# Two pairs of late token tiles multiplied in seven half-width products instead of eight

## The chip, the cores and the metric

The kernel runs on one core of a Trainium2 chip. The metric is the device time of one execution in microseconds (us). Before the change the median of three runs is 405.96 us (405.43 to 406.44). A profiled execution, with its trace, lies beside them.

## The reference

Eight batches of 576 tokens pass two stages. The first is attention through 32 packed queries, with 8 heads of 64 columns: `packed = softmax(p k^T / 8) v`, then `out = softmax(q packed^T / 8) packed`. The second is a gated feed-forward layer on the 512 columns that the heads make together:

```python
h = np.maximum(x @ w_in, 0.0)                  # 512 -> 1024
conv_out = sum(conv_w[k] * hp[:, k:k + S, :])  # three neighbouring tokens, per column
gate = 1.0 / (1.0 + np.exp(-conv_out))
return h * gate @ w_out                        # 1024 -> 512
```

The last line is the second layer. The change is in that product alone: 4608 tokens by 1024 columns of `h * gate`, times `w_out` of 1024 by 512. Results are float32, and q, k, p and `conv_w` are drawn eight times larger than plain random numbers.

## The kernel before

**Precision.** TensorE multiplies rounded float32 (`F32R`). Each operand x of a product is split into `hi`, x rounded, and `lo`, x minus `hi`. A product is three matmuls into one PSUM tile: hi by hi, lo by hi, hi by lo. ScalarE (ACT) writes `hi`, VectorE (DVE) writes `lo`.

**First layer.** `ffn1(b, j)` (L645) computes 128 of the 1024 columns for batch b: 12 matmuls of 288 columns (L666) into a `big` PSUM tile, of which there are three. Then ACT and DVE take turns on 576 tokens: relu out of PSUM (L678), the convolution's middle tap (L682), its two outer taps (L684, L688 on DVE), tanh (L692) and the gating (L694 on DVE), which leaves `hgt[b % 2][:, j]`.

**Second layer.** `ffn2(m)` (L715), for each of the 36 tiles of 128 tokens: ACT and DVE convert the tile's 1024 columns of `hgt` into `xhi` and `xlo` (L705, L708), PE takes 8 steps of three matmuls of 512 columns (L757), ACT copies the PSUM tile to `o` (L765) and SP's queue stores it (L767). There are two `x` pairs and two `o` tiles. The PSUM tile is `fo`, or `sm` for odd m from 31 on. The last tile is done in two halves of 256 columns, `sm` and then `fo`. Tiles 29 and 30 hold tokens of batch 6 alone, tile 31 of batches 6 and 7, tiles 32 to 35 of batch 7 alone.

**Order.** Each function is a stream of steps, one step for one engine. `ORDER` is a fixed string of two-character stream numbers: `Flow.run` (L156) takes them in turn and emits the next step of that stream. So the order of the instructions on each engine is fixed by the string, and the engines meet only at semaphores. The planner's times in the steps decide nothing here except how many idle matmuls fill the start. Tiled steps (AV, scores, `packed_weight`) use parts of the array, the others all of it.

Of the kernel before, what the change touches and what calls it, by code (L numbers as in the profile page):

```python
# [26 lines left out]
    "1a0u1n0m0u124f6e1n451l4d4e4f6e0u454f4d1a4h1c4e4e0u0u4f4g1b0y1k4d451b4i4f4f114j4i7e1n7e4k4i6e1g4h6f4j6e6e4i6f6e4k"  # L27
    "4h4k4i4j4i7f161i121a4k4j4i6e1i6f6f121e1a4j4k4l7f1d126f6f6f6f4j4k4l1i6f1o4k6g121s4l1i4l6g4h124l7g4m1a4l6f1a1j4m1q"
    "191j1i1a6f4m4j121i6g1q7g1w6g6h6e4n6g4m6h1q204n1a1v6g1i6g4m1v4l1h6g4m1a4n124m121r1v4n6g6g236f7h1a6g4o121i4n1i4o4p"
    "6h6h4o4p4p1a236h124o7h4o6h4n1q6g4p1a6h6h6h4p6h4o1m4o1a1y4n234p4p1q1i6h1i1q4q282b1y4r6i1r1y6i1y1a1i6i126i6i1q1a2b"  # L30
    "4r6i12241a4q4q1z6i6j1a6i1a4r1i6i6i4s6i2b1p4s6j4s1q4t4u1q4s1i1y1i4t4s264t1t4t1q1z6k1y2g6j2c4u6j1y4u4s261i6j2j4u6j"
    "4s6k6j264u2j4v4t2j1q6j271i4u1u4v226i4u6j266j4t2e1x4w2k6j4t1i4v1q2e1i1q6k4w2e4v2a1i1q6h2f2e4v3p6k6k6k4w1y1i274x26"
    "6k1q6k6l1y4x6l216k6k6k2f4x1q6k4x2m1y4v50266m1q6l6l4w264v1q2r2m6l2h4w6l2m2r506l4x2r6l4y4w1q4y291y6l6l4w501q4y6l6m"
    "4z6m4z262o2n4x1q6m4z2e6m4y6m6m2z1y4x4z6m264y4y4z524z1y4y52524z6l6m251y522s6m34536n535354542e6m2m542e26512u526n6n"
    "6o6n546j6n261y516n532z54526n2z6n6n6n52541y376n516o376p5554553753536m6o262u6o2w552e5630266o6o55266o5635535655266o"
    "6o57552n5756551y56566o2i6p6o1y586p262u6p586q562e596p262d58596p6p6n596p2m6p1y586p6q58576p2m2e6o2u57595a1y5732592m"
    "6q2l1y58586q57266q596q6q3232572m3f2m6q362q6q592e266r6q5b6q262m6r3f2e265a5b6r6r6s6p6r6r5a5c2m6r6s2e5d6r6r5c2e6r5c"
    "5d2m5b5c5c5d5e6r2m6s2e5c6s5e325c5f2u2e5d5e5e6r5d5d383f5e5f2e6s5f5e336s6s6t2v5f6s6s2e6t5k3a2m5d2p2u6s5f5f6s5k5g6t"
# [146 lines left out]
def tile_packed_attention_conv_gate(  # L185
# [15 lines left out]
    HG = 4  # L201
# [17 lines left out]
    MOVED = 10  # L219

# [7 lines left out]
    stage = cpool.tile([128, 2 * DFF], F32, name="stage")  # L228
    cw_raw = cpool.tile([3 * NJ, 128], F32, name="cw_raw")
    cw = cpool.tile([128, 3 * NJ], F32, name="cw")  # L230
    w_in_sb = cpool.tile([128, NCC, DFF], F32, name="w_in_sb")
# [8 lines left out]
    vfree = [cpool.tile([128, HG, SV + 1, D], F32, name=f"v{i}") for i in range(2)]  # L240
# [3 lines left out]
    def warm(n):  # L244
# [6 lines left out]
        | dict(gw=2, h=3, x=2, o=2),  # L251
# [4 lines left out]
    def big():  # L256
        return ps.tile([128, 2, 512], F32, name="big", tag="big", bufs=3)

# [230 lines left out]

    afree = [stage[:, i * (SV + 1) * 128 : (i + 1) * (SV + 1) * 128] for i in range(2)]  # L490

    def attention(g):
# [12 lines left out]
        if g >= MOVED:  # L505
            yield Step("DVE", 1230, after=[("wp", 2), ("wp", 5)], take=["ad"], give=["a1"])
# [28 lines left out]
        yield Step("PE", 640, after=[("v", g)], take=["sm"], give=["a1T", "v"], cols=960, tiled=True)  # L535
# [12 lines left out]
        vfree.append(G["v"])  # L548
        yield Step("ACT", 251, after=[("rs", g)], take=["pb"], give=["sm"], sets=[("pb", g)])
# [10 lines left out]
        yield Step("PE", 556, after=[("qT", g)] + [("s2", g - 1)] * (g > 0), take=["big", "s2"], give=["qT"], sets=[("s2", g)], cols=1152, tiled=True)  # L560
        t = score(ppT, G["qT"], g)
        yield Step("DVE", 665, give=["big"])
# [41 lines left out]
    def packed_weight(b, hf):  # L604
# [3 lines left out]
        yield Step("PE", 905, after=after, take=["big", "gw"], give=["ppT"] * NG if hf else (), sets=[("pk", i)], cols=2048, tiled=True)  # L608
        t = big()
        for i in range(NG * HG):  # L610
# [11 lines left out]
            )  # L622
        yield Step("ACT", 904)
# [18 lines left out]

    hfree = list(hbuf)

    def ffn1(b, j):  # L645
# [3 lines left out]
        if b >= 2:  # L649
            after += [("x", m) for m in tiles_of(b - 2)]  # L650
# [64 lines left out]
    def ffn2(m):  # L715
        bs = range(m * 128 // S, ((m + 1) * 128 - 1) // S + 1)
        halves = m < HALVED
        last = NJ // 2 if halves else NJ
        after = [("hg", b, j) for b in bs for j in range(last)]
        if m:  # L720
            after.append(("x", m - 1))
        yield Step("ACT", 520 if halves else 947, after=after, take=["x"])
        hi = wk.tile([128, NJ, 128], F32R, name="xhi", tag="xhi")
        lo = wk.tile([128, NJ, 128], F32R, name="xlo", tag="xlo")
        cuts = []
        for b in bs:
            s0, s1 = max(m * 128, b * S), min((m + 1) * 128, (b + 1) * S)
            cuts.append((hgt[b % 2][:, :, s0 - b * S : s1 - b * S], slice(s0 - m * 128, s1 - m * 128)))
        split[m] = hi, lo, cuts
        yield from convert(m, slice(0, last), [("xa" if halves else "x", m)])  # L730
        bank = "sm" if m > NTT - 6 and m % 2 else "fo"
        parts = 2 if m == NTT - 1 else 1
        banks = ("sm", "fo") if parts == 2 else (bank,)
        for n in range(NJ * parts):
            q, c = divmod(n, NJ)
            fs = slice(q * DM // parts, (q + 1) * DM // parts)
            end = n == NJ * parts - 1
            after = [("w", 4 + c // 2)]
            if n == 0 and m:
                after.append(("fo", m - 1))  # L740
            if c == last:
                after.append(("x", m))
# [6 lines left out]
                give=["x"] if end else (),  # L749
# [3 lines left out]
            if c == 0:  # L753
                t = small(banks[q])
                sums_of[m, q] = t
            for i, (x, w) in enumerate(((hi, wo_hi), (lo, wo_hi), (hi, wo_lo))):
                nc.tensor.matmul(  # L757
                    out=t[:, : fs.stop - fs.start], lhsT=x[:, c, :], rhs=w[:, c, fs], start=c + i == 0, stop=c == NJ - 1 and i == 2
                )
        yield from store(m, fs, q, banks[q])  # L760

    def store(m, fs, q, bank):
# [4 lines left out]
        nc.sync.dma_start(out=out.rearrange("b s f -> (b s) f")[m * 128 : (m + 1) * 128, fs], in_=o[:, fs])  # L767

# [21 lines left out]
    for m in range(NTT):  # L790
        flow.add(ffn2(m))
# [34 lines left out]
```

## Time and profile before

| | us |
|---|---|
| median of three runs | 405.96 |
| the profiled execution's own time | 408.01 |
| its span, first to last instruction | 406.2 |
| PE busy | 395.3 (97%) |
| DVE busy | 339.9 (84%) |
| ACT busy | 275.5 (68%) |

The profile is one execution. PE is TensorE's matmuls, PEld its weight loads, SPq the queue of transfers that SP issues. A matmul's shown duration overlaps the next one's start, so what one costs is read from start to start. Every mean granted clock is 1.000, which is 2.4 GHz. The chain of waits follows the work back from the last instruction, and before the last store it is PE alone from 369 us on. Three things are to be kept apart: how long PE's own work is, what PE waited for, and how far ahead of it DVE and ACT were.

### The profile page before, as it was taken

Reading aid. Unit: us, or ns where it says so; the run is one execution under the profiler, and the core shown is the slowest. Engines: PE = TensorE matmul, PEld = TensorE weight load, DVE = VectorE, ACT = ScalarE, POOL = GpSimd, SP = SyncE. Lnnn points to the kernel's source line nnn. Section 1 sums busy time; section 2 is a strip of 40 time slices with the busy share of each in tenths; the row PEclk is TensorE's granted clock in tenths of the full one; section 3 lists DMA queues with packets and bytes.
Section 4 is the critical chain, followed back from the end, with each engine's and each line's share of the span. In section 5 each row is a group of like instructions: output and inputs, shape, how many; then the busy total and the mean of one; then the engine's idle time right before and its main releaser. Section 6 shows DMA issues by size and latency. Waiting matters only on the chain.

```text
span 406.2 us, 8244 instructions
## 1 busy us (share of the span) xinstructions
PE 395.3 (97%) x3321; PEld 316.9 (78%) x3321; DVE 339.9 (84%) x494; ACT 275.5 (68%) x475; POOL 1.6 (0%) x16
## 2 busy tenths in 40 slices
PE   7899899999999999999999999999999999999996
PEld 5768576778868878888779788788687878887886
DVE  0699989999999999999999999999889886557220
ACT  3889899977777586776666765677665676655231
POOL 1000000000000000000000000000000000000000
PEclk9999999999999999999999999999999999999999
DMA  8999989999758787397473715416001001010211
GB/s 295 363 353 209 319 225 176 134 155 158 111 92 118 118 192 142 73 190 113 92 114 102 148 54 102 129 31 114 28 2 52 27 6 47 26 53 0 77 53 52
DMA packets 140377, 49.19 MB, mean 121 GB/s; under 512 B 121244, under 2 KB 132788, under 8 KB 140340
## 3 DMA queue, kind: packets, MB, share of 16 engines
q1 hardware_dynamic: 140340, 48.67, 54.5%
q8 instruction: 26, 0.43, 0.5%
q14 instruction: 11, 0.09, 0.1%
HBM read 37.25 MB, written 9.44 MB: 115 GB/s over the span
## 4 chain that ended last, share of the span: by engine, by line
PE 79%; DMA 10%; DVE 5%; SPq 3%; ACT 2%; issue 1%; ACTq 0%
PE fo L757 42%; PE big L666 20%; DMA v<-in_v_dram 4%; PE sm L757 3%; PE big L453 3%; DMA hgt<-in_moe_w_in_dram 3%; PE big L614 3%; SPq L520 2%; PE sm L539 2%; DMA p<-in_p_dram 1%; PE big L331 1%; PE big L530 1%; DMA out_dram<-o 1%; DVE hgt L684 1%; DVE hgt L688 1%
## 5 line engine op out<-in xcount | busy, mean ns | idle before, releaser
L757 PE MATMUL fo<-wo_hi,xhi 128*128 128x512 f32 (+1 forms) x272 | 109.8, 404 | 0.7 <-ACT o L765 0.7
L757 PE MATMUL fo<-wo_lo,xhi 128*128 128x512 f32 (+1 forms) x272 | 106.5, 391 | 0.0
L757 PE MATMUL fo<-wo_hi,xlo 128*128 128x512 f32 (+1 forms) x272 | 106.1, 390 | 0.0
L757 PEld LDWEIGHTS fo<-wo_hi,xhi 128*128 128x128 f32 x272 | 51.2, 188 | 15.7 <-issue 3.0
L678 ACT ACTIVATE hbuf<-big 128x576 f32<-128x576 f32 x64 | 41.7, 657 | 31.5 <-PE big L666 31.4
L684 DVE SCALAR_TENSOR_TENSOR hgt<-hbuf,cw,hgt 128x576 f32<-128x576 f32 x64 | 51.3, 806 | 13.4 <-ACT hgt L682 13.0
L757 PEld LDWEIGHTS fo<-wo_lo,xhi 128*128 128x128 f32 x272 | 51.1, 188 | 12.3
L708 DVE TENSOR_TENSOR xlo<-hgt,xhi 128x1024 fp32r<-128x1024 f32 (+1 forms) x44 | 44.7, 1021 | 16.7 <-ACT xhi L705 16.6
L757 PEld LDWEIGHTS fo<-wo_hi,xlo 128*128 128x128 f32 x272 | 51.1, 188 | 8.6
L666 PE MATMUL big<-a2hi,ghi 128*128 128x288 f32 x256 | 55.7, 299 | 0.0
L692 ACT ACTIVATE hgt<-hgt 128x576 f32<-128x576 f32 x64 | 43.7, 688 | 16.7 <-DVE hgt L688 16.4
L666 PE MATMUL big<-a2hi,glo 128*128 128x288 f32 x256 | 54.3, 294 | 0.0
L666 PE MATMUL big<-a2lo,ghi 128*128 128x288 f32 x256 | 54.2, 293 | 0.0
L688 DVE SCALAR_TENSOR_TENSOR hgt<-hbuf,cw,hgt 128x576 f32<-128x576 f32 x64 | 50.8, 804 | 0.4
L694 DVE SCALAR_TENSOR_TENSOR hgt<-hgt,hbuf 128x576 f32<-128x576 f32 x64 | 47.3, 745 | 4.6 <-ACT hgt L692 4.3
L682 ACT ACTIVATE hgt<-hbuf,cw 128x576 f32<-128x576 f32 x64 | 49.8, 782 | 0.9
L666 PEld LDWEIGHTS big<-a2hi,ghi 128*128 128x128 f32 x256 | 42.9, 188 | 5.8 <-ACT glo L634 0.8
L705 ACT CAST xhi<-hgt 128x1024 fp32r<-128x1024 f32 (+1 forms) x44 | 38.9, 890 | 11.0 <-PE fo L757 6.6
L765 ACT COPY o<-fo 128x512 f32<-128x512 f32 (+1 forms) x34 | 19.7, 579 | 33.0 <-PE fo L757 26.9
L666 PEld LDWEIGHTS big<-a2lo,ghi 128*128 128x128 f32 x256 | 40.9, 188 | 0.0
L666 PEld LDWEIGHTS big<-a2hi,glo 128*128 128x128 f32 x256 | 40.8, 188 | 0.0
L498 DVE TENSOR_REDUCE nm<-big 128x1 f32<-128x576 f32 x16 | 12.0, 747 | 12.0 <-PE big L453 12.0
(93 smaller groups left out, 489.9 us busy)
## 6 DMA issues: line engine op xcount, KB each, us to landing
out_dram<-o SPq DMA_DIRECT2D x35, 256.0 KB, 2.7
v<-in_v_dram SPq DMA_DIRECT2D x16, 512.0 KB, 6.1
k<-in_k_dram SPq DMA_DIRECT2D x48, 144.0 KB, 4.3
q<-in_q_dram SPq DMA_DIRECT2D x48, 144.0 KB, 4.0
hgt<-in_moe_w_in_dram SPq DMA_DIRECT2D x3, 1024.0 KB, 10.8
hgt<-in_moe_w_out_dram SPq DMA_DIRECT2D x3, 1024.0 KB, 7.0
a1T<-stage SPq DMA_DIRECT2D x96, 20.0 KB, 1.8
hgt<-in_k_dram SPq DMA_DIRECT2D x2, 576.0 KB, 5.4
```

The source lines that it names most:

```text
L453: nc.tensor.matmul(out=o.rearrange("c (j r) -> c j r", r=NR) if by_block(g) else o, lhsT=lhs[r, 32 * i : 32 * i + 32], rhs=rhs[r, :, h, :] ...
L666: nc.tensor.matmul(out=t[:, hf, :SH], lhsT=w[:, gg, js], rhs=x[:, hf * SH : (hf + 1) * SH], start=n == 0, stop=n == 3 * NG - 1,)
L678: nc.scalar.activation(out=h[:, 1 : S + 1].rearrange("c (f s) -> c f s", f=2), in_=t[:, :, :SH], func=AF.Relu, scale=0.5)
L682: nc.scalar.activation(out=d, in_=h[:, 1 : S + 1], func=AF.Copy, scale=cw[:, NJ + j : NJ + j + 1])
L684: nc.vector.scalar_tensor_tensor(out=d, in0=h[:, 0:S], scalar=cw[:, j : j + 1], in1=d, op0=ALU.mult, op1=ALU.add)
L688: nc.vector.scalar_tensor_tensor(out=d, in0=h[:, 2 : S + 2], scalar=cw[:, 2 * NJ + j : 2 * NJ + j + 1], in1=d, op0=ALU.mult, op1=ALU.add)
L692: nc.scalar.activation(out=d, in_=d, func=AF.Tanh)
L694: nc.vector.scalar_tensor_tensor(out=d, in0=d, scalar=1.0, in1=h[:, 1 : S + 1], op0=ALU.add, op1=ALU.mult)
L705: nc.scalar.copy(out=hi[:, js, o], in_=src[:, js])
L708: nc.vector.tensor_tensor(out=lo[:, js, o], in0=src[:, js], in1=hi[:, js, o].bitcast(F32), op=ALU.subtract)
L757: nc.tensor.matmul(out=t[:, : fs.stop - fs.start], lhsT=x[:, c, :], rhs=w[:, c, fs], start=c + i == 0, stop=c == NJ - 1 and i == 2)
L765: nc.scalar.copy(out=o[:, fs], in_=sums_of[m, q][:, : fs.stop - fs.start])
```

## The change

Tiles 29 and 30, and tiles 32 and 33, are each taken together as a 256 by 1024 matrix, cut into blocks A11, A12 (first tile, columns 0 to 511 and 512 to 1023) and A21, A22 (second tile). `w_out` is cut the same way into four quarters B of 512 by 256. Strassen's scheme in Winograd's form needs seven block products instead of eight, with these sums:

- of tokens, for each pair: S1 = A21 + A22, S2 = S1 - A11, S3 = A11 - A21, S4 = A12 - S2
- of weights, once: T1 = B12 - B11, T2 = B22 - T1, T3 = B22 - B12, T4 = T2 - B21
- products: A11 B11, A12 B21, S1 T1, S2 T2, A22 T4, S4 B22, S3 T3

Each product is 12 matmuls of 256 columns. The products lie in four half-banks of two PSUM tiles, a `big` one (bank 0) and `sm` (bank 1). S2 and S3 accumulate on the half of A11, S4 on that of S1. `results` copies partial results out with ACT in between (four copies of 256 columns for a pair), and two adds on DVE and two stores finish the two output tiles. Tile 31 and the last two are converted in halves by `load_block`; the other tiles below 29 run as before. All tiles but the last now use `fo`. SBUF room for the new blocks is what first-stage tiles leave (`stage`, `w_in`, `v`, `kq`, `kT`, `qT`, `a1`, `a1T`).

`ORDER` is another string from its 645th step on, in the middle of tile 7. Read from it, PE's steps at the end are: first layer (7, 6), A11 of pair 29, first layer (7, 7), one step of tile 31, A12, three steps of tile 31, S1, S2, A11 of pair 32, A22, S4, S3, four steps of tile 31, A12 of pair 32, tile 34, S1, S2, A22, S4, S3 of pair 32, tile 35. The number of first-layer, score, AV, transpose and `packed_weight` steps is unchanged.

```diff
+    PAIRS = (29, 32)
+    BLOCKED = min(PAIRS)
+    BANKS = {m: ("big", "sm") for m in PAIRS}
...
+    def lasts(m):
         parts = 2 if m == NTT - 1 else 1
-        banks = ("sm", "fo") if parts == 2 else (bank,)
+        return ("sm", "fo") if parts == 2 else ("fo",)
...
-        bank = "sm" if m > NTT - 6 and m % 2 else "fo"
...
+    def load_block(m, k):
+        js = slice(4 * k, 4 * k + 4)
+        after = [("hg", b, j) for b in batches_of(m) for j in range(js.start, js.stop)]
+        yield Step("ACT", 520, after=after, take=["xb"])
+        hi, lo = blocks[m, k] = xfree.pop(0)
+        for src, o in cuts_of(m):
+            nc.scalar.copy(out=hi[:, :, o], in_=src[:, js])
+        yield Step("DVE", 601, sets=[("x", m, k)])
+        for src, o in cuts_of(m):
+            nc.vector.tensor_tensor(out=lo[:, :, o], in0=src[:, js], in1=hi[:, :, o].bitcast(F32), op=ALU.subtract)
...
+    def combined(m, key):
+        whole = lambda k: wholes[m, k]
+        after, op, late, pair = dict(
+            S1=(gates(m, 0, 1), ALU.add, [("xf", m, "S2")], lambda: (half_tile(m + 1, 0), half_tile(m + 1, 1))),
+            S2=([("xf", m, "S1")], ALU.subtract, [("xf", m, "S4")], lambda: (whole("S1"), half_tile(m, 0))),
+            S3=(gates(m, 0), ALU.subtract, [], lambda: (half_tile(m, 0), half_tile(m + 1, 0))),
+            S4=([("xf", m, "S2")], ALU.subtract, [], lambda: (half_tile(m, 1), whole("S2"))),
+        )[key]
+        yield Step("DVE", 601, after=after, take=["s2"], sets=[("xf", m, key)])
+        x, y = pair()
+        full = wholes[m, key] = rows_of(wk.tile([128, S], F32, name="s2", tag="s2", bufs=2)[:, :512])
+        nc.vector.tensor_tensor(out=full, in0=x, in1=y, op=op)
+        yield Step("ACT", 520, take=["xb"])
+        hi, lo = blocks[m, key] = xfree.pop(0)
+        nc.scalar.copy(out=hi, in_=full)
+        yield Step("DVE", 601, after=late, give=["s2"], sets=[("xr", m, key)])
+        nc.vector.tensor_tensor(out=lo, in0=full, in1=hi.bitcast(F32), op=ALU.subtract)
...
+    def products(m):
+        for key, w, after, bank, at, first in (
+            ("A11", lambda: quarters(0, 0), [], 0, 0, True),
+            ("A12", lambda: quarters(1, 0), [], 1, 0, True),
+            ("S1", lambda: sums_w["T1"], [("T", "T1")], 1, 256, False),
+            ("S2", lambda: sums_w["T2"], [("T", "T2"), ("kept", m, "A11")], 0, 0, False),
+            ("A22", lambda: sums_w["T4"], [("T", "T4")], 0, 256, False),
+            ("S4", lambda: quarters(1, 1), [("kept", m, "S1")], 1, 256, False),
+            ("S3", lambda: sums_w["T3"], [("T", "T3"), ("kept", m, "S2"), ("kept", m, "A22")], 0, 0, False),
+        ):
+            yield Step(
+                "PE",
+                12 * 119,
+                after=[("xr", m, key)] + after,
+                take=[BANKS[m][bank]] if first else (),
+                give=["xb"],
+                sets=[("P", m, key)],
+                cols=3072,
+            )
+            if first:
+                turns[m, bank] = bank_of(BANKS[m][bank])
+            hi, lo = blocks[m, key]
+            whi, wlo = w()
+            for c in range(4):
+                for i, (x, y) in enumerate(((hi, whi), (lo, whi), (hi, wlo))):
+                    nc.tensor.matmul(
+                        out=turns[m, bank][:, at : at + 256],
+                        lhsT=x[:, c, :],
+                        rhs=y[:, c, :],
+                        start=first and c + i == 0,
+                        stop=c == 3 and i == 2,
+                        skip_group_check=True,
+                    )
+            xfree.append(blocks[m, key])
...
+    def results(m, i):
+        one, two = (("A11", 0, 0, "A11"), ("S2", 0, 0, "A22")) if i == 0 else (("S1", 1, 256, "S1"), ("A22", 0, 256, "A22"))
+        for n, (key, bank, at, last) in enumerate((one, two)):
+            fs = slice(256 * (n ^ i), 256 * (n ^ i) + 256)
+            yield Step("ACT", 263, after=[("P", m, last)], take=["o"] * (n == 0), sets=[("kept", m, key)])
+            if n == 0:
+                o = wk.tile([128, DM], F32, name="o", tag="o")
+            nc.scalar.copy(out=o[:, fs], in_=turns[m, bank][:, at : at + 256])
+        last = ("P", m, "S3" if i else "S4")
+        yield Step("DVE", 601, after=[last], give=[BANKS[m][1 - i]])
+        parts = o.rearrange("r (c n) -> r c n", c=2)
+        if i:
+            more = turns[m, 0][:, :256].unsqueeze(1).broadcast_to([128, 2, 256])
+        else:
+            more = turns[m, 1].rearrange("r (c n) -> r c n", c=2)
+        nc.vector.tensor_tensor(out=parts, in0=parts, in1=more, op=ALU.add)
+        yield Step("SP", 730, give=["o"])
+        nc.sync.dma_start(out=out.rearrange("b s f -> (b s) f")[(m + i) * 128 : (m + i + 1) * 128, :], in_=o)
...
+    def weight_sum(key):
+        others, first, second, take, kept = dict(
+            T1=(["wf", "T3"], "T3", "T1", ["v", "v"], [("ws", "T2")]),
+            T3=(["wf", "T2"], "T2", "T3", ["wi"], []),
+            T2=(["ws", "T3"], "T2", "T1", ["ad", "ad"], [("ws", "T4"), ("T", "T1")]),
+            T4=(["ws", "T2"], "T4", "T2", ["wi"], [("T", "T2")]),
+        )[key]
...
+        after = [("wf", key), tuple(others)] + [("ws", "T1")] * (key in ("T2", "T3"))
+        yield Step("DVE", 1135, after=after, sets=[("ws", key)])
+        full = fulls[key]
+        nc.vector.tensor_tensor(out=full, in0=fulls[first], in1=fulls[second], op=ALU.subtract)
```

## Rows read from the trace of the kernel before

**Rows 1.** The page, engines' busy times and the span in 40 equal slices.

```profile
span 406.2 us, 8244 instructions
PE 395.3 (97%) x3321; PEld 316.9 (78%) x3321; DVE 339.9 (84%) x494; ACT 275.5 (68%) x475; POOL 1.6 (0%) x16
...
DVE  0699989999999999999999999999889886557220
...
PEclk9999999999999999999999999999999999999999
```

**Rows 2.** Windows from 152 us: length, then busy PE, PEld, DVE, ACT, POOL.

```profile
152.00:270.00 118.00, 117.72 (x988) 95.71 (x987) 116.08 (x166) 80.11 (x136) 0.00 (x0) 1.00 0.55 111
270.00:320.00 50.00, 50.00 (x368) 40.89 (x367) 45.64 (x66) 33.94 (x55) 0.00 (x0) 1.00 0.20 48
320.00:375.00 55.00, 54.33 (x298) 45.57 (x297) 38.20 (x48) 32.19 (x48) 0.00 (x0) 1.00 0.07 24
375.00:406.00 31.00, 28.06 (x144) 23.52 (x142) 4.90 (x4) 7.40 (x11) 0.00 (x0) 1.00 0.16 60
```

**Rows 3.** PE's waits, 152 to 406 us: total us, times, longest.

```profile
PE fo L757 <- ACT o L765: 0.7, 1, 0.7
PE sm L539 <- DMA a1T<-stage: 0.3, 1, 0.3
```

**Rows 4.** The chain that ended last, in order of time: start, us, what.

```profile
368.40 0.59 ACT o L765
...
374.90 5.60 PE sm L757 x24
...
397.30 2.88 PE sm L757 x24
400.18 2.89 PE fo L757 x24
```

**Rows 5.** PE's timeline: start, us, line, operation, shapes.

```profile
153.83 0.27 PE L480 MATMUL sm<-ident,pm 128*128 128x128 f32 x1
153.85 0.48 PE L757 MATMUL fo<-wo_hi,xhi 128*128 128x512 f32 x1
154.17 0.41 PE L757 MATMUL fo<-wo_hi,xlo 128*128 128x512 f32 x1
...
367.97 0.40 PE L757 MATMUL fo<-wo_lo,xhi 128*128 128x512 f32 x1
369.04 0.49 PE L757 MATMUL fo<-wo_hi,xhi 128*128 128x512 f32 x1 [0.67 <-ACT o L765]
```

**Rows 6.** DVE's timeline, back to back, and two half-tile conversions.

```profile
148.59 1.22 DVE L708 TENSOR_TENSOR xlo<-hgt,xhi 128x1024 fp32r<-128x1024 f32 x1
149.72 0.16 DVE L602 RECIPROCAL rs<-rs 128x1 f32<-128x1 f32 x1
...
149.86 0.81 DVE L684 SCALAR_TENSOR_TENSOR hgt<-hbuf,cw,hgt 128x576 f32<-128x576 f32 x1
150.59 0.26 DVE L581 RECIPROCAL sm<-sm 128x18 f32<-128x18 f32 x1
...
151.40 0.75 DVE L694 SCALAR_TENSOR_TENSOR hgt<-hgt,hbuf 128x576 f32<-128x576 f32 x1
152.07 0.75 DVE L583 TENSOR_TENSOR s<-s,sm 128x576 f32<-128x576 f32 x1
...
371.64 1.46 DVE L708 TENSOR_TENSOR xlo<-hgt,xhi 128x512 fp32r<-128x512 f32 x2
```

**Rows 7.** ACT's timeline: a half-tile conversion and a 256-column copy.

```profile
371.76 0.62 ACT L705 CAST xhi<-hgt 128x512 fp32r<-128x512 f32 x1 [0.32 <-DVE hgt L694]
...
400.26 0.37 ACT L765 COPY o<-sm 128x256 f32<-128x256 f32 x1 [2.29 <-PE sm L757]
```

**Rows 8.** Stores after 330 us: time from issue to landing.

```profile
L767 SPq DMA_DIRECT2D out_dram<-o x13: 332/332/434, 334.1 to 403.5; - x13
...
DMA to landing us min/median/max: 1.7/2.0/4.1
```

More of the change, by code (lines that the diff above doesn't have):

```diff
@@ L505, in attention @@
         if g >= MOVED:
-            yield Step("DVE", 1230, after=[("wp", 2), ("wp", 5)], take=["ad"], give=["a1"])
+            yield Step("DVE", 1230, after=[("wp", 2), ("wp", 5)], take=["ad"], give=["a1"] * (g < NGT - 1))
             blocks = afree.pop(0)
@@ L534, in attention @@
             a1T = a1T.rearrange("r s (h n) -> r h s n", h=HG)
-        yield Step("PE", 640, after=[("v", g)], take=["sm"], give=["a1T", "v"], cols=960, tiled=True)
+        end = g == NGT - 1
+        yield Step("PE", 640, after=[("v", g)], take=["sm"], give=["xb" if end else "a1T", "v"], cols=960, tiled=True)
         t = small()
@@ L548, in attention @@
         vfree.append(G["v"])
+        if end:
+            xfree.append(
+                block(
+                    wk.tile([128, (SV + 1) * 128], F32R, name="a1T", tag="a1T", bufs=1),
+                    wk.tile([128, S], F32R, name="a1", tag="a1", bufs=1),
+                )
+            )
         yield Step("ACT", 251, after=[("rs", g)], take=["pb"], give=["sm"], sets=[("pb", g)])
@@ L559, in attention @@
         nc.scalar.copy(out=ppT, in_=t[:, :128])
-        yield Step("PE", 556, after=[("qT", g)] + [("s2", g - 1)] * (g > 0), take=["big", "s2"], give=["qT"], sets=[("s2", g)], cols=1152, tiled=True)
+        yield Step("PE", 556, after=[("qT", g)] + [("s2", g - 1)] * (g > 0), take=["big", "s2"], give=["xb" if end else "qT"], sets=[("s2", g)], cols=1152, tiled=True)
         t = score(ppT, G["qT"], g)
+        if end:
+            xfree.append(block(wk.tile([128, HG * SH], F32R, name="qT", tag="qT", bufs=1)))
         yield Step("DVE", 665, give=["big"])
@@ L622, in packed_weight @@
             )
+        if hf and b == B - 1:
+            t2 = wk.tile([128, NCC * DFF], F32R, name="sums", tag="w_in", bufs=1)
+            homes["T3"], homes["T4"] = t2[:, :2048], t2[:, 2048:]
         yield Step("ACT", 904)
@@ L641, in tiles_of, with in_pair, converted @@
         return range(b * S // 128, -(-(b + 1) * S // 128))
+    def in_pair(m):
+        return m in PAIRS or m - 1 in PAIRS
+    def converted(m):
+        if in_pair(m):
+            first = m if m in PAIRS else m - 1
+            return [("xr", first, k) for k in ("A11", "A12", "S1", "S2", "S3", "S4", "A22")]
+        return [("x", m)] if m < BLOCKED else [("x", m, k) for k in range(2)]
     hfree = list(hbuf)
@@ L736, in ffn2 @@
             fs = slice(q * DM // parts, (q + 1) * DM // parts)
+            after = [("w", 4 + c // 2)] + (ready(c) if q == 0 else [])
+            if n == 0 and m and not in_pair(m - 1):
+                after.append(("fo", m - 1))
             end = n == NJ * parts - 1
[L738 to L742, printed above, removed]
             sets = [("fo", m, q)] * (c == NJ - 1) + [("fo", m)] * end + ["second"] * (m + n == 0)
@@ L755, in ffn2, with ready, give, used @@
                 sums_of[m, q] = t
+            hi, lo = tile_of(c)
             for i, (x, w) in enumerate(((hi, wo_hi), (lo, wo_hi), (hi, wo_lo))):
                 nc.tensor.matmul(
-                    out=t[:, : fs.stop - fs.start], lhsT=x[:, c, :], rhs=w[:, c, fs], start=c + i == 0, stop=c == NJ - 1 and i == 2
+                    out=t[:, : fs.stop - fs.start], lhsT=x, rhs=w[:, c, fs], start=c + i == 0, stop=c == NJ - 1 and i == 2
                 )
+            used(n, end)
         yield from store(m, fs, q, banks[q])
+    def ffn2(m):
+        halves = m < HALVED
+        last = NJ // 2 if halves else NJ
+        after = [("hg", b, j) for b in batches_of(m) for j in range(last)]
+        if m:
+            after.append(("x", m - 1))
+        yield Step("ACT", 520 if halves else 947, after=after, take=["x"])
+        hi = wk.tile([128, NJ, 128], F32R, name="xhi", tag="xhi")
+        lo = wk.tile([128, NJ, 128], F32R, name="xlo", tag="xlo")
+        split[m] = hi, lo, cuts_of(m)
+        yield from convert(m, slice(0, last), [("xa" if halves else "x", m)])
+        def ready(c):
+            return [("xa" if halves else "x", m)] if c == 0 else [("x", m)] * (c == last)
+        def give(n, end):
+            if not end:
+                return ()
+            return ["xb"] * 2 if m >= BLOCKED - 2 else ["x"]
+        def used(n, end):
+            if end and m >= BLOCKED - 2:
+                xfree.extend((hi[:, js], lo[:, js]) for js in (slice(0, NJ // 2), slice(NJ // 2, NJ)))
+        yield from multiply(m, lambda c: (hi[:, c, :], lo[:, c, :]), ready, give, used)
@@ new lines, in ffn2_blocks, with ready, give, used @@
+    def ffn2_blocks(m):
+        def ready(c):
+            return [("x", m, c // 4)] * (c % 4 == 0)
+        def give(n, end):
+            if m == NTT - 1:
+                return ()
+            return ["xb"] * (n % 4 == 3)
+        def used(n, end):
+            if m < NTT - 1 and n % 4 == 3:
+                xfree.append(blocks[m, n // 4])
+        yield from multiply(m, lambda c: [a[:, c % 4, :] for a in blocks[m, c // 4]], ready, give, used)
+    blocks = {}
+    turns = {}
+    def load_block(m, k):
[8 more added lines that the diff above has]
+            nc.vector.tensor_tensor(out=lo[:, :, o], in0=src[:, js], in1=hi[:, :, o].bitcast(F32), op=ALU.subtract)
@@ L767, in store, with quarters, half_tile, gates @@
         nc.sync.dma_start(out=out.rearrange("b s f -> (b s) f")[m * 128 : (m + 1) * 128, fs], in_=o[:, fs])
+    def quarters(k, n):
+        return [w[:, 4 * k : 4 * k + 4, 256 * n : 256 * n + 256] for w in (wo_hi, wo_lo)]
+    def half_tile(m, k):
+        ((src, _),) = cuts_of(m)
+        return src[:, 4 * k : 4 * k + 4]
+    def gates(m, *ks):
+        (b,) = batches_of(m)
+        return [("hg", b, j) for k in ks for j in range(4 * k, 4 * k + 4)]
+    def plain(m, key, t, k):
+        yield Step("ACT", 520, after=gates(m, k), take=["xb"])
+        hi, lo = blocks[m, key] = xfree.pop(0)
+        src = half_tile(m + t, k)
+        nc.scalar.copy(out=hi, in_=src)
+        yield Step("DVE", 601, sets=[("xr", m, key)])
+        nc.vector.tensor_tensor(out=lo, in0=src, in1=hi.bitcast(F32), op=ALU.subtract)
@@ new lines, in tile_packed_attention_conv_gate, with whole_quarter @@
+    sums_w = {}
+    fulls = {}
+    def whole_quarter(key, k, n):
+        after, tag = [("w", 4 + 2 * k), ("w", 5 + 2 * k)], "kT" if key == "T3" else "kq"
+        before = dict(T2="T1", T4="T2").get(key)
+        yield Step("DVE", 1135, after=after + [("wf", before)] * bool(before), take=[tag], sets=[("wf", key)])
+        t = wk.tile([128, KQ], F32, name=tag, tag=tag, bufs=1 if tag == "kT" else 3)
+        full = fulls[key] = rows_of(t[:, :1024])
+        x, y = quarters(k, n)
+        nc.vector.tensor_tensor(out=full, in0=x.bitcast(F32), in1=y.bitcast(F32), op=ALU.add)
@@ new lines, in weight_sum @@
+    def weight_sum(key):
[9 more added lines that the diff above has]
+        nc.vector.tensor_tensor(out=full, in0=fulls[first], in1=fulls[second], op=ALU.subtract)
+        yield Step("ACT", 905, take=take)
+        if key == "T1":
+            hi, lo = (
+                wk.tile([128, HG * (SV + 1) * D], F32R, name="sum", tag=f"v{i}", bufs=1)[:, :1024] for i in range(2)
+            )
+        else:
+            if key == "T2":
+                homes[key] = wk.tile([128, 2 * DFF], F32R, name="sum", tag="stage", bufs=1)
+            hi, lo = homes[key][:, :1024], homes[key][:, 1024:]
+        hi, lo = sums_w[key] = rows_of(hi), rows_of(lo)
+        nc.scalar.copy(out=hi, in_=full)
+        yield Step("DVE", 1135, after=kept, give=["xb"], sets=[("T", key)])
+        nc.vector.tensor_tensor(out=lo, in0=full, in1=hi.bitcast(F32), op=ALU.subtract)
+        tag = "kT" if key == "T3" else "kq"
+        xfree.append(block(wk.tile([128, KQ], F32R, name=tag, tag=tag, bufs=1 if tag == "kT" else 3)))
@@ L790, in tile_packed_attention_conv_gate @@
     for m in range(NTT):
-        flow.add(ffn2(m))
+        if not in_pair(m):
+            if m < BLOCKED:
+                flow.add(ffn2(m))
+            else:
+                flow.add(ffn2_blocks(m))
+                for k in range(2):
+                    flow.add(load_block(m, k))
+    for m in PAIRS:
+        for key, t, k in (("A11", 0, 0), ("A12", 0, 1), ("A22", 1, 1)):
+            flow.add(plain(m, key, t, k))
+        for key in ("S1", "S2", "S3", "S4"):
+            flow.add(combined(m, key))
+        flow.add(products(m))
+        for i in range(2):
+            flow.add(results(m, i))
+    for key, k, n in (("T3", 0, 1), ("T1", 0, 0), ("T2", 1, 1), ("T4", 1, 0)):
+        flow.add(whole_quarter(key, k, n))
+        flow.add(weight_sum(key))
     for m in range(HALVED):
```

91 lines of the change are left out of this document (50 added, 41 removed).

## The prediction

> **What bounds the kernel now.** I read the page's busy times and slices first: PE is busy 97% of the span at a full granted clock, DVE 84%, and DVE's slices fall from 9 to 2 only in the last quarter [rows 1]. Then the windows: from 152 us, the step from which the order differs, to 406 us PE is busy for all but the last store, while DVE idles 1.9 of 118 us up to 270, 4.4 of the next 50 and 16.8 of the 55 after those [rows 2]. The list of waits says what PE stood for in that stretch: two waits, 0.7 and 0.3 us [rows 3]. The chain that ended last is PE alone from 369 us on [rows 4]. So PE's own work sets the end, one for one, and DVE runs close behind it until about 320 us. Two questions decide: how much PE work goes, and whether DVE and ACT can still feed it.
>
> **PE's work.** A whole tile is 24 matmuls of 512 columns in 5.60 us, so 0.233 us each from start to start. The last tile is done in halves of 256 columns: 24 matmuls in 2.88 us, so 0.120 us each, weight load included and hidden [rows 4]. A block product is 12 of those, 1.44 us. A pair cost 2 x 5.60 = 11.20 us and will cost 7 x 1.44 = 10.08. Two pairs: -2.24 us. All of it lies on the path.
>
> One rule of the Trainium skill prices this otherwise. The rows show 0.120 and 0.233 us [rows 4]; the page "TensorE: Matmul & The Clock Gate", section "Wait — 56ns, not 53.3ns?", says that a matmul of N columns costs N / 2.4 GHz plus about 2.5 ns, which an estimate from that page makes 0.109 and 0.216 us, and the two pairs 2 x (48 x 0.216 - 84 x 0.109) = 2.4 us cheaper. The trace disagrees with its level by 8 to 10%, and the sum stays with the rows.
>
> **The wait that goes.** Tile 30 follows tile 29 directly and both use `fo`. PE's last matmul of 29 starts at 367.97 and the first of 30 at 369.04, 1.07 us later instead of 0.23: ACT's copy of `fo` lay between. The first matmul after a break takes about 0.1 more, as from 153.85 to 154.17 [rows 4, 5]. In the new order only tiles 31 and 34 both use `fo` late, with a product of 1.44 us between, and the last tile starts in `sm`. I take -0.9, bounds 0 (ACT late by 0.5 us) and -0.94. All other neighbouring tiles have a first-layer step or tiled steps between them.
>
> **Smaller changes of the order.** A transpose alone among full matmuls delays the next one: 0.32 instead of 0.23 us to the following start [rows 5]. From the 645th step on, ten stood alone and eight will; the others join groups of tiled steps, whose number stays nine. I take -0.2, bounds -0.2 and 0. The 0.3 us wait for a transfer of `a1T` [rows 3] may go or stay: the shortest distance between two AV steps grows, counted over PE's steps, from 14.8 to 18.0 us. I leave it in: 0, bounds -0.4 (with the 0.1 of a break) and +0.4 (a second one like it).
>
> **What is added beside PE.** Start to start, DVE needs 1.13 us for 1024 columns, 0.73 for a tap, 0.67 for a gating; two half-tile conversions lasted 1.46 us and I take 0.6 for one [rows 6]. The whole conversions of tiles 29 to 35 go (7 x 1.13 = 7.9). There come 12 whole-width operations for T1 to T4 (13.6), 12 half-width `lo` of plain blocks (7.2), 8 sums and 8 `lo` for S1 to S4 (9.6) and 4 adds out of PSUM, which the trace doesn't show; between 0.6 as SBUF's half-width and 1.13 as a whole-width operation I take 0.65 (2.6). Together +25 us of DVE. It is hidden only if it fits ahead of PE's due times. ACT gains some 8 us and idles much more than that [rows 2].
>
> The tightest place is S3 of pair 29, for which T3's `lo` comes last. Up to it, summed over DVE's steps in the written order from the 645th step on, DVE has 213.8 us to do (200.5 was the whole rest before; the seven conversions go, the twelve operations of the T and thirteen half-width ones lie ahead of it). PE reaches S3 after the same work as before up to tile 30's end at 374.9 [rows 4], less 0.9 and 0.2, less 11.2 for tiles 29 and 30, plus half of tile 31 (2.8) and seven products (10.1): 375.5 us. From 152.3 that is 223 us, so DVE may idle 9 us, 4%. It idled 1.6% up to 270 us. The 8.7% after that [rows 2] fell where the old order had nothing due; the sums T wait for no other engine and can fill it. So I cost DVE's work at nothing, and what it costs without that cover is a rival below.
>
> **New waits.** Where a half-bank is read before PE may add to it, another product lies between. S3 waits for two ACT copies of 256 columns that start when A22 ends: at most 0.2 to start (368.20 to 368.40), 2 x 0.37 and 0.05 back, 1.0 us, against S4's 1.44 [rows 4, 5, 7]. Behind these copies ACT's queue holds the conversions of A12 of pair 32 and of tile 31's second half. The latter's chain from A22's end: 1.0, two conversions of 0.62, DVE's 0.73 and 0.3 of signals make 3.2 us, against S4 and S3's 2.88 [rows 6, 7]. So tile 31's fifth step comes some 0.3 late at worst, and I take +0.3 for all new waits together. Bounds 0 and 2 (six such hand-overs, each 0.3 late).
>
> The `o` tiles are held longer: a pair keeps both until its adds are stored. The copy of S1 in pair 32 needs the `o` of tile 34. From tile 34's end: 0.2, 0.6 for the copy, a landing of 2.0, the copy's 0.4 and 0.1, 3.3 us, against three products, 4.3. With the longest landing, 4.1, it is 1.1 late [rows 8]; this I keep for the range.
>
> **Sum.** -2.24 - 0.9 - 0.2 + 0.3 = -3.0 us. The profiled execution's span of 406.2 becomes 403.2, and its own 408.0 becomes 405.0. That execution is 2.0 above the median of the runs, 405.96, from which the same difference gives **403.0 us**. Without new waits and with the `a1T` wait gone it is -3.8: 402.2.
>
> **Rivals.**
>
> *Hand-overs late in the tail.* One mechanism: a product finishes and ACT is inside another instruction, so the copy that frees the half-bank starts up to a half-tile conversion later (0.6), and the slack of 0.4 at S3 and S4 turns into waits. For it: in-order ACT, 0.4 us of slack, landings up to 4.1 [rows 8]. Against: ACT idled 41% of the time from 320 to 375 us [rows 2]. Four of six late by 0.2 and one landing late by 1.1: +1.9 in place of +0.3, 404.6 us.
>
> *DVE becomes the bound: slower.* Its place is the stretch from 270 us to S3. With an idle share s there, DVE is late by 1.9 + 105 x s - 9 us. At the 8.7% of the window 270 to 320 [rows 2] it is 2.1 late: 405.1 us. It decides from about 10%, where nothing is left of the gain; at 14% it is 7.6 late, 410.6 us. For it: each S needs a DVE sum, an ACT copy and a DVE subtraction, so DVE can stand waiting for ACT. Against: sums of other blocks stand between in the written order, and, summed step by step over both engines, the old order had DVE's work due within 1 us of PE at eight places before 270 us, where PE lost 0.3 [rows 3]; in the new one the closest are 1.0 us in tile 8 and 3.6 in tile 25.
>
> *Half-width products don't stream.* If the weight load, not the 256 columns, set the pace, at PE's weight loads' mean of 316.9 / 3321 = 0.095 us to the 0.120 seen nothing changes [rows 1, 4]; a switch between products that costs a break of 0.1 each makes 14 x 0.1: 404.4 us. Against: 24 half-width matmuls pass from `sm` to `fo` at 400.18 with no break [rows 4].
>
> **How the numbers follow.** What can be told from no change is about 0.3%, 1.2 us: faster is under 404.7, slower over 407.2. Forecast 70% (402.2 to 403.9); late hand-overs 13%; DVE late 12%, half of it within 0.3% or a little faster and half slower; no streaming 4%; 1% else. From these: faster 0.82 (forecast, most of the hand-overs, a few of the others), same 0.10, slower 0.08. The range reaches from 402.2 to 405.1, which takes in the hand-overs and DVE at its old idle share.
>
> **What would show it.** In the new profile: the products' line at 0.120 us from start to start; no wait of PE for ACT's copy at 368 us; PE's last matmul of the first layer and those after it without gaps over 0.5 us; DVE's slices at 9 to about 375 us, then falling. Wrong if PE shows waits for DVE's `lo` of a T or an S after 330 us, or a sum of waits over 2 us.

## The result, and the profile after

The changed kernel's median is 402.56 us (401.95 to 403.46) against 405.88 for the kernel before: a ratio of 0.9919, with a 95% interval of 0.9893 to 0.9946. That is 3.3 us less. A second set of rounds gave 402.50 against 406.43, 0.9910 (0.9892 to 0.9928). The forecast was 403.0 us, 3.0 us less.

The page's busy times and DVE's slices, as in [rows 1]:

```profile
span 400.2 us, 8463 instructions
PE 392.2 (98%) x3393; PEld 318.8 (80%) x3393; DVE 365.5 (91%) x532; ACT 284.1 (71%) x497; POOL 1.6 (0%) x16
...
DVE  0789999999999999999999999999999999999751
```

DVE has 26 us more to do, and its last quarter, where the slices fell from 9 to 0 before, is full almost to the end. The windows show the same stretches as [rows 2] (length, busy PE, PEld, DVE, ACT, POOL, then the granted clock):

```profile
152.00:270.00 118.00, 118.00 (x983) 95.63 (x982) 115.75 (x165) 79.15 (x133) 0.00 (x0) 1.00 0.53 101
270.00:320.00 50.00, 50.00 (x367) 40.74 (x366) 48.68 (x64) 33.75 (x52) 0.00 (x0) 1.00 0.24 59
320.00:375.00 55.00, 55.00 (x354) 48.98 (x353) 52.91 (x74) 41.40 (x68) 0.00 (x0) 1.00 0.07 26
375.00:400.00 25.00, 22.10 (x155) 20.35 (x153) 10.60 (x17) 7.16 (x15) 0.00 (x0) 0.99 0.20 74
```

PE has no idle time from 152 us to its end: both waits of [rows 3] are gone, and the list of PE's waits over that stretch is empty. DVE idled 16.8 us between 320 and 375 and now idles 2.1. The chain that ended last shows the products (start, us, engine, PSUM tile, line, matmuls; L926 is the products' line, L794 the second layer's):

```profile
358.87 1.43 PE big L926 x12
360.30 1.59 PE big L705 x12
361.89 0.70 PE fo L794 x3
362.59 1.43 PE sm L926 x12
364.02 2.09 PE fo L794 x9
366.11 1.42 PE sm L926 x12
367.53 4.23 PE big L926 x36
371.76 1.41 PE sm L926 x12
373.17 1.41 PE big L926 x12
374.59 2.80 PE fo L794 x12
377.38 1.43 PE sm L926 x12
378.82 5.59 PE fo L794 x24
384.41 1.37 PE sm L926 x12
385.78 2.84 PE big L926 x24
388.62 1.43 PE sm L926 x12
390.05 1.43 PE big L926 x12
391.48 2.81 PE sm L794 x24
394.30 2.82 PE fo L794 x24
```

Each row begins where the one above ends. The seven products of a pair stand there among tiles 31 and 34 without a gap, twice.

The two profiled spans, 406.2 and 400.2 us, differ by 6.0, more than the medians. The rest lies in the first 150 us, where both kernels run the same order: the first differing step of PE starts at 152.4 us before and at 150.2 after, since waits for transfers in the first 50 us fell out differently in these two executions. From that step to PE's end it is 250.6 us before and 246.9 after, 3.7 us less. Measured from tile 7's first matmul, 1.5 us earlier, to PE's end it is 252.13 and 248.45 us, and a second profiled execution of the changed kernel has 248.45 too. So this stretch, called the late stretch below, tells small differences better than the medians do. Summed from start to start over PE's rows, the 3.7 us are:

| PE's time from the 645th step on | us |
|---|---|
| four whole tiles (22.40) against fourteen products (19.84) | -2.56 |
| the wait for `fo` between tiles 29 and 30, with the slow restart | -0.94 |
| all tiled steps and transposes (19.98 against 19.77), the wait of 0.3 for `a1T` among them | -0.2 |
| last tile's halves (2.88 + 2.89 against 2.81 + 2.82) | -0.13 |
| first layer and the other whole tiles | +0.15 |

The AV steps alone took 0.6 less, but a matmul's row from start to start takes in the break behind it, and other tiled steps stand last in some of the groups now; these took 0.4 more.

### The profile page after: what moved, and what is told of

It is laid out like the page before. It is cut to its first block, busy times and chain, and to the rows that moved or that the text cites. A ratio compares the mean times of both kernels' runs of the same rounds, so it can differ in the third digit from the quotient of the medians.

```text
span 400.2 us, 8463 instructions
## 1 busy us (share of the span) xinstructions
PE 392.2 (98%) x3393; PEld 318.8 (80%) x3393; DVE 365.5 (91%) x532; ACT 284.1 (71%) x497; POOL 1.6 (0%) x16
## 4 chain that ended last, share of the span: by engine, by line
PE 84%; ACT 8%; DMA 5%; SPq 1%; issue 1%
PE fo L794 44%; PE big L705 23%; PE big L460 3%; PE big L641 3%; DMA q<-in_q_dram 3%; PE big L926 3%; DMA v<-in_v_dram 2%; PE sm L926 2%; PE sm L557 2%; ACT hgt L731 1%; ACT hgt L721 1%; PE big L547 1%; ACT hgt L275 1%; ACT glo L664 1%; SPq L404 1%; PE sm L794 1%
## 5 line engine op out<-in xcount | busy, mean ns | idle before, releaser
L794 PE MATMUL fo<-wo_hi,xhi 128*128 128x512 f32 x240 | 97.9, 408 | 0.0
L794 PE MATMUL fo<-wo_lo,xhi 128*128 128x512 f32 x240 | 94.8, 395 | 0.0
L794 PE MATMUL fo<-wo_hi,xlo 128*128 128x512 f32 x240 | 94.5, 394 | 0.0
L794 PEld LDWEIGHTS fo<-wo_hi,xhi 128*128 128x128 f32 x240 | 45.3, 189 | 13.3 <-issue 2.5
L794 PEld LDWEIGHTS fo<-wo_lo,xhi 128*128 128x128 f32 x240 | 45.1, 188 | 11.2
L794 PEld LDWEIGHTS fo<-wo_hi,xlo 128*128 128x128 f32 x240 | 45.1, 188 | 7.9
L747 DVE TENSOR_TENSOR xlo<-hgt,xhi 128x1024 fp32r<-128x1024 f32 (+1 forms) x36 | 35.8, 1002 | 0.0
L858 ACT COPY o<-fo 128x512 f32<-128x512 f32 (+1 forms) x32 | 18.5, 580 | 21.2 <-PE fo L794 19.6
L744 ACT CAST xhi<-hgt 128x1024 fp32r<-128x1024 f32 (+1 forms) x36 | 31.5, 881 | 2.2 <-DVE hgt L733 2.2
```

What stands on the lines that cost most here:

```text
L744: nc.scalar.copy(out=hi[:, js, o], in_=src[:, js])
L747: nc.vector.tensor_tensor(out=lo[:, js, o], in0=src[:, js], in1=hi[:, js, o].bitcast(F32), op=ALU.subtract)
L794: nc.tensor.matmul(out=t[:, : fs.stop - fs.start], lhsT=x, rhs=w[:, c, fs], start=c + i == 0, stop=c == NJ - 1 and i == 2)
L858: nc.scalar.copy(out=o[:, fs], in_=sums_of[m, q][:, : fs.stop - fs.start])
```

## The experiments

All are timed against the kernel before, in the same rounds. Differences from the changed kernel compare the two ratios to the kernel before; their intervals reach some 1.2 us to either side. Beside them stands the late stretch of the profiled execution, against 248.45 us of the changed kernel or, where the kernel before was edited, 252.13. Line numbers of the experiments differ by a few from those of the changed kernel.

**The wait for `fo` alone.** The kernel before, with another PSUM tile for tile 29:

```diff
-        bank = "sm" if m > NTT - 6 and m % 2 else "fo"
+        bank = "sm" if m > NTT - 8 and m % 2 else "fo"
```

> The kernel before, with tile 29's sums in the sm tile instead of fo, so that tile 30 no longer waits for ACT's copy. If that wait of 0.84 us (0.94 with the slower start behind it) is on the path and is one part of the gain, the time falls by 0.9 us, from 405.9 to 405.0, and PE goes from tile 29 to tile 30 without a gap. If ACT or DVE would have held tile 30 anyway, it stays at 405.9 and the gap comes back under another name.

Measured: 405.26 against 406.16 us, 0.9976 (0.9961 to 0.9991), 1.0 us less. In the late stretch it is 1.2 us less, 0.2 of them at an AV step that waited 0.3 us for `a1T` before and 0.1 here. The chain passes from tile 29 to tile 30 without a gap, where the kernel before had 1.07 us from one matmul to the next [rows 5]:

```profile
363.98 2.10 PE sm L757 x9
366.08 5.60 PE fo L757 x24
```

So this part of the gain needs no Strassen at all. One changed number has it.

**Eight products in the new order.**

```diff
-            for c in range(4):
+            for c in [*range(4)] * (2 if key == "A11" else 1):
```

> The changed kernel with A11's product of each pair done twice, so that PE has eight half-width products for a pair again and all else stays. If PE alone sets the end, it grows by 2 x 1.42 = 2.8 us, from 402.6 to 405.4, which gives back about what the seven products saved. If DVE or ACT already set the pace in the last 50 us, PE's added work falls into their time and the growth is under 1.4 us.

Measured: 405.92 against 406.16 us, 0.9988 (0.9975 to 1.0001), 3 us more than the changed kernel, with no wait of PE. The late stretch is 2.81 us longer. An eighth product comes back one for one: 2 x 1.42 = 2.8. So the seventh of eight products, not another order of the rest, is the larger part of the gain, and neither DVE nor ACT set the pace.

**Half-width by itself.** The kernel before, with both halves of a step in one bank:

```diff
+            if m in (29, 30, 32, 33):
+                for h in range(2):
+                    hs = slice(256 * h, 256 * h + 256)
+                    for i, (x, w) in enumerate(((hi, wo_hi), (lo, wo_hi), (hi, wo_lo))):
+                        nc.tensor.matmul(
+                            out=t[:, hs], lhsT=x[:, c, :], rhs=w[:, c, hs], start=c + i + h == 0,
+                            stop=c == NJ - 1 and i == 2, skip_group_check=True,
+                        )
+                continue
```

> The kernel before, with tiles 29, 30, 32 and 33 multiplied in halves of 256 columns, 96 matmuls more in all, nothing else changed. It prices half-width by itself. At the 0.1175 us from start to start that the changed kernel's products show, 4 x (48 x 0.1175 - 24 x 0.2333) = +0.2 us: 406.1. At the forecast's 0.120 it is +0.6: 406.5. With a break of 0.1 us at each switch between the halves, +6: 412.

Measured: 406.58 against 405.99 us, 1.0022 (1.0007 to 1.0037), 0.6 us more. Two rows of its chain, one tile in halves and one whole:

```profile
384.29 5.76 PE sm L760 x48
390.05 5.61 PE fo L766 x24
```

48 half-width matmuls take 5.76 us here, 0.120 each. The late stretch is 0.55 us longer. From the old `x` tiles and `w_out` the forecast's price was right. The products are cheaper, 0.114 to 0.121. The changed kernel's timeline of PE has two that follow each other, from the same kind of `x` block; the third row is the next product's first:

```profile
368.78 0.28 PE L926 MATMUL big<-wo_hi,xhi 128*128 128x256 f32 x1
...
370.23 0.28 PE L926 MATMUL big<-sums,xhi 128*128 128x256 f32 x1
...
371.60 0.28 PE L926 MATMUL sm<-wo_hi,a1T 128*128 128x256 f32 x1
```

A11 of the second pair, on a quarter of `w_out` itself, took 1.45 us, and A22 of the first, on a sum of weights, 1.37. The weights alone don't decide it: S2 of the first pair, on a sum of weights too, and S4, on a quarter of `w_out`, both took 1.41. Whether the place of the operands in SBUF or their stride makes the difference was not tried.

**More work for DVE.** Four, eight and one operation of 1024 columns more, where `hi` and `lo` of the weight quarters are added up. This is the edit for four; for eight it says `range(3)`, for one `range(2 if key == "T1" else 1)`:

```diff
-        nc.vector.tensor_tensor(out=full, in0=x.bitcast(F32), in1=y.bitcast(F32), op=ALU.add)
+        for _ in range(2):
+            nc.vector.tensor_tensor(out=full, in0=x.bitcast(F32), in1=y.bitcast(F32), op=ALU.add)
```

> The changed kernel with four more DVE operations of 1024 columns (1.13 us each, 4.5 us): each of the four whole weight quarters is added up twice. They lie at about 290 to 320 us. If DVE may idle 9 us up to S3 of the first pair, as forecast, the time stays at 402.6. By the trace of the changed kernel DVE idles only some 2 us from there to S3 and T3's lo is done 0.6 us before S3: then about 2 us come through, 404.6. If DVE were already the bound, all 4.5: 407.1.

> The same with eight more DVE operations (9.0 us). With the forecast's 9 us of room the time is 402.6 to 403. With about 2.5 us of room, as the trace of the changed kernel shows, 6.5 come through: 409.1. Had DVE no room at all, 411.6. The difference from the run with four is 4.5 us if the room is used up by then.

Measured: with four, 406.41 against 406.16 us, 1.0009 (0.9992 to 1.0025), 3.6 us more than the changed kernel; with eight, 412.56, 1.0156 (1.0135 to 1.0177), some 9.6 us more. The late stretch is 4.3 and 9.8 us longer. Both expectations were too low: 2 and 6.5. PE's timeline with four shows where (in brackets: idle time and releaser), and the windows below it what followed (the clock is the third number from the right):

```profile
312.25 0.49 PE L794 MATMUL fo<-wo_hi,xhi 128*128 128x512 f32 x1 [1.08 <-ACT o L858]
313.90 0.50 PE L794 MATMUL fo<-wo_hi,xlo 128*128 128x512 f32 x1 [1.16 <-DVE xlo L747]
```

```profile
312.00:314.00 2.00, 0.59 (x2) 0.28 (x2) 2.00 (x3) 1.53 (x3) 0.00 (x0) 1.00 0.35 131
314.00:316.00 2.00, 2.00 (x6) 1.62 (x7) 2.00 (x3) 0.00 (x0) 0.00 (x0) 0.63 0.00 0
316.00:318.00 2.00, 2.00 (x6) 1.36 (x5) 1.97 (x5) 0.00 (x0) 0.00 (x0) 0.52 0.00 0
318.00:320.00 2.00, 2.00 (x35) 0.77 (x34) 1.82 (x4) 1.77 (x3) 0.00 (x0) 1.00 0.00 0
```

Tile 24 waited twice: for ACT's copy of tile 23, which stood behind ACT's conversions of T1 and T2, and for its own `lo`. Both are 2.2 us, and 2.7 with the signals and the slow restart. Behind these two waits the granted clock fell to half, 1.2 GHz, and eight matmuls of 512 columns took 0.38 to 0.43 instead of 0.233 us from start to start: 1.5 us more. That makes up the 4.3. With eight operations PE waited 0.9 us for a `lo` at 305 us, then 3.7 and 1.2 at tile 24, and the clock fell too. It doesn't fall each time: with four, seven of the twelve timed runs kept a mean granted clock of 1.000 (median 406.34 us), and five show 0.994 to 0.996 as the profiled one does (406.75). So DVE work added there comes through at tile 24, long before S3, and a late operation can cost nearly twice its wait; how much of the 3.6 us timed is the clock's stays open. In the changed kernel's own trace the lead there is small:

```profile
308.44 1.22 DVE L747 TENSOR_TENSOR xlo<-hgt,xhi 128x1024 fp32r<-128x1024 f32 x1
```

```profile
309.24 0.59 ACT L858 COPY o<-fo 128x512 f32<-128x512 f32 x1
```

```profile
310.61 0.39 PE L794 MATMUL fo<-wo_hi,xhi 128*128 128x512 f32 x1
```

The `lo` ends at 309.66 and the copy at 309.83. PE needs them at 310.84 and 310.61: 1.2 and 0.8 us ahead. With one operation more this lead should just do.

> The changed kernel with one DVE operation of 1024 columns (1.13 us) more: only the first weight quarter is added up twice, at about 295 us. In the changed kernel's trace tile 24's lo and ACT's copy of tile 23 are done some 1.0 us before PE comes to tile 24. If that lead is what DVE has, one operation is just covered and the time is that of the changed kernel within 0.3 us, where four cost 3.6. If every added DVE operation comes through, +1.1.

Measured: 402.89 against 402.50 for the changed kernel in the same rounds (0.9927, 0.9905 to 0.9949, against 0.9910). The intervals overlap, and an effect of 1.1 us can't be excluded by the time alone. In the list of PE's waits there is none, but tile 24's first matmuls show a small one:

```profile
312.52 1.22 DVE L747 TENSOR_TENSOR xlo<-hgt,xhi 128x1024 fp32r<-128x1024 f32 x1
```

```profile
313.43 0.39 PE L794 MATMUL fo<-wo_hi,xhi 128*128 128x512 f32 x1
313.79 0.50 PE L794 MATMUL fo<-wo_hi,xlo 128*128 128x512 f32 x1
314.13 0.40 PE L794 MATMUL fo<-wo_lo,xhi 128*128 128x512 f32 x1
```

The `lo` ends at 313.74, and the second matmul, which reads it, starts 0.36 us behind the first instead of 0.23; the third is 0.1 late, as behind a break. The late stretch is 0.28 us longer. So the operation's 1.13 us are covered but for 0.13: the room at tile 24 is 1.0 us.

**DVE directly before S3.**

```diff
-        nc.vector.tensor_tensor(out=lo, in0=full, in1=hi.bitcast(F32), op=ALU.subtract)
+        for _ in range(2 if key == "T3" else 1):
+            nc.vector.tensor_tensor(out=lo, in0=full, in1=hi.bitcast(F32), op=ALU.subtract)
```

> The changed kernel with the lo of T3 written twice (1.13 us of DVE more at 371 us, directly before the product S3 of the first pair). By the trace it is done 0.6 us before S3 needs it, and the chain to tile 31's fifth step has 0.35 us. So PE should wait about 0.5 us there: +0.5. If DVE has the 9 us that were forecast for S3, 0.

Measured: 403.90 against 402.50 in the same rounds (0.9950, 0.9931 to 0.9969). The one new wait of PE in its trace:

```profile
373.65 0.62 PE L926 MATMUL big<-sums,kq 128*128 128x256 f32 x3 [0.30 <-DVE sums L992]
```

S3's third matmul comes 0.46 us later than its stream would have it, as expected: of the operation's 1.13 us, 0.67 was covered. The late stretch is 0.55 us longer, the slow restart behind the wait included. The medians differ by 1.4 us, which the intervals stretch from about 0.5 to 2.7. Two of the ten runs had a mean granted clock of 0.996 and 0.992 and took 406.42 and 405.79; the eight others have a median of 403.53. What is left beyond 0.55, no wait of PE shows.

**S3 directly behind A22.** The last two products of the second pair change places, and in `ORDER` the last copy stands before both:

```diff
+            *(
                 ("S4", lambda: quarters(1, 1), [("kept", m, "S1")], 1, 256, False),
                 ("S3", lambda: sums_w["T3"], [("T", "T3"), ("kept", m, "S2"), ("kept", m, "A22")], 0, 0, False),
+            )[:: -1 if m == 32 else 1],
```

> The changed kernel with the last two products of the second pair in the other order: S3 directly behind A22, on whose half-bank ACT's two copies must first be done, and S4 last. If the product between hides the hand-over of a half-bank, S3 now waits some 0.9 us, and the last tile waits some 1.0 us for sm, which is free only after the add behind S4: 402.6 + 1.9 = 404.5 us. If hand-overs cost nothing to speak of, it stays at 402.6.

Measured: 404.73 against 405.99 us, 0.9973 (0.9959 to 0.9987), 2 us more than the changed kernel; the late stretch is 2.15 us longer. PE's timeline has the two waits:

```profile
389.38 1.71 PE L928 MATMUL big<-sums,kq 128*128 128x256 f32 x12 [0.74 <-ACT o L945]
...
393.36 0.50 PE L794 MATMUL sm<-wo_hi,qT 128*128 128x256 f32 x2 [0.84 <-DVE o L953]
```

From start to start they cost 0.90 and 0.99 us. A hand-over of a half-bank costs what was forecast, 1.0, and one product between hides it.

**One PSUM tile for both banks.**

```diff
-                take=[BANKS[m][bank]] if first else (),
+                take=["big"] if first and bank == 0 else (),
-            if first:
-                turns[m, bank] = bank_of(BANKS[m][bank])
+            if first and bank == 0:
+                both = big()
+                turns[m, 0], turns[m, 1] = both[:, 0, :], both[:, 1, :]
-        yield Step("DVE", 601, after=[last], give=[BANKS[m][1 - i]])
+        yield Step("DVE", 601, after=[last], give=["big"] * i)
```

> The changed kernel with both half-bank pairs of a pair of tiles in the two banks of one big PSUM tile, instead of one bank of a big tile and the sm tile. If waits follow the bank that is read and written, nothing changes: 402.6 us. If they follow the PSUM tile, ACT's copies out of one bank hold PE's products into the other: up to three waits of about 1.0 us in each pair, 404 to 408 us.

Measured: 408.89 against 405.99 us, 1.0062 (1.0042 to 1.0082): slower than the kernel before, and 6 us more than the changed kernel. PE waits five times for ACT's copies, 3.6 us in all. Three of the five:

```profile
374.34 0.38 PE L927 MATMUL big<-wo_hi,a1T 128*128 128x256 f32 x1 [0.74 <-ACT o L944]
...
390.45 0.39 PE L927 MATMUL big<-sum,a1T 128*128 128x256 f32 x1 [1.82 <-ACT o L944]
...
396.19 1.71 PE L927 MATMUL big<-sums,kq 128*128 128x256 f32 x12 [0.46 <-ACT o L944]
```

At 374.34 S4 of the first pair waits for copies out of the other bank. At 390.45 S2 of the second pair waits for the copy of S1, which reads the other bank too and itself waited 1.6 us for an `o` to be stored. So the waits follow the PSUM tile, not the bank, and the products' order hides a copy only when the two half-bank pairs are two tiles. The Trainium skill's page "PSUM — Partial Sum Buffer", section "PSUM bank collisions raise a hardware error", asks for semaphores by bank; here they came for the whole tile, as these rows show. From start to start the five cost 4.4 us, and the late stretch is 5.0 us longer with the slow restarts behind them. In this profiled execution the granted clock was also 0.70 and 0.87 in two stretches of 4 us from 20 us on, with no such dip in the changed kernel's. The run with the eighth product has one as well (0.58 from 20 to 24 us), and up to 150 us all three have the same order, so nothing ties it to this edit. Two of the six runs kept a mean clock of 1.000, with 407.11 and 407.84 us, some 5 above the changed kernel; the four others, at 0.996, took 408.83 to 409.51. So some 5 of the 6 us are the waits'.

## Why the prediction was right, step by step

**PE alone sets the end.** Right: no wait of PE from 150 us on, and an eighth product comes back one for one, 2.81 of 2.84 us in the late stretch.

**Seven products for eight.** The mechanism was right, and the size was off by 0.3: -2.24 forecast, -2.56 in the trace. A product took 1.42 us on average, not 1.44. The old tiles in halves do cost 0.120 a matmul; the new blocks do not. The estimate from the Trainium skill's page "TensorE: Matmul & The Clock Gate", section "Wait — 56ns, not 53.3ns?", was -2.4, between the two; its price of a matmul of 256 columns, 0.109 us, is below every one seen.

**The wait for `fo`.** Right: -0.9 forecast, -0.94 in the trace, and -1.0 when it was taken away alone.

**Smaller changes of the order.** The size was right, its source in part another: -0.2 forecast, and -0.2 in all for tiled steps, transposes, first layer, the other whole tiles and the last tile's halves. The `a1T` wait went, which the forecast had kept; this was its bound of -0.4. The breaks of about 0.1 us between kinds of full matmuls and transposes or tiled steps are 26 instead of 28 from the 645th step on, and 2.4 us in all instead of 2.6. What took back some 0.4 of these two isn't located; some rows are missing in either trace.

**New waits.** +0.3 forecast, 0 measured. Tile 31's fifth step was to be late by 0.3 at worst. From the start of S4 at 371.60, right behind A22, to the end of that tile's `lo` at 374.07 it was 2.5 us, where the forecast had 3.2 with its signals, and PE came to that step at 374.43: ACT's copies follow each other at 0.26 us and its conversions at 0.52, not at their full durations. Of the 3.7 us in the late stretch, against 3.0 forecast, these 0.3 and the products' 0.3 are nearly all of the difference.

**DVE's room.** The amount of work was right: 25 us more forecast, 25.6 on the page. The forecast cost it at nothing, and that held, but in part by luck, for its reason was wrong in size and missed a place. It gave DVE 9 us of room up to S3 and put the tightest place there; its step-by-step sum named tile 8 with 1.0 us and tile 25 with 3.6 as the closest. The runs showed 0.67 us at S3, and 1.0 us at tile 24, which it had not named and where four operations of 1.13 us were already 3.6 us too much. Of the 9 us, DVE idled 4.8 on the way (from 150.2 us to the end of T3's `lo` at 372.39 it was busy 217.4 of 222.2), 2.3 of them waiting for ACT's middle tap. The rest isn't separated: at 150.2 us DVE still had earlier steps in front of it, and some work may have been priced too low. The sum of DVE's work against PE's time leaves out such waits, and those of ACT: its conversions of T1 and T2, 2 us with one short copy between, stood before the copy that frees `fo`. The rival "DVE becomes the bound" was therefore nearer than its 12%, and can be dearer: it counted the lateness alone and not the clock's fall behind it, 1.5 us in the profiled run with four operations.

**Hand-overs late in the tail.** This rival's price of a hand-over was right (0.9 and 1.0 where the cover was taken away) and its condition didn't arise: the copy of S1 in pair 32 waited 1.6 us for its `o` and still ended 0.9 us before S4 began.

## What to carry to other kernels

When one engine is busy all the time, instructions taken from it count one for one, and a sum over its rows forecasts the time. Whether the others still feed it isn't answered by a sum of their work: look at each place for how long before its use a result is ready, and at what stands ahead of the copy that frees a buffer on an in-order queue. Partial results that one engine reads while another goes on writing belonged, here, in separate PSUM tiles, with work on the other tile between a write, its copy and the next write.

## What the runs showed that I had not expected

Two waits of PE, of 1.1 and 1.2 us close together, were followed in the profiled run by a granted clock of 0.63 and 0.52 in the next two stretches of 2 us, which cost 1.5 us more: a small lateness of DVE can cost nearly double, though by their mean clock seven of that kernel's twelve timed runs had no such fall. And blocks of the same shape, streamed back to back, took 1.37 to 1.45 us for twelve matmuls of 256 columns, by which operands they read.
